# Attention with decay and a cosine feed-forward on one core: the order of all operations taken from a written table, buffers given out in that order

## The chip, the core and the metric

The kernel runs on one core of a Trainium2 chip. A core has a matrix engine (TensorE, PE in the profile, with its weight loads as PEld), a vector engine (VectorE, DVE), a scalar engine (ScalarE, ACT), a general engine (GpSimd, POOL) and a queue that starts transfers (SyncE, SP). Every engine runs its own list of instructions strictly in the order in which they were issued, and waits by semaphores for the others. The metric is the time of one execution on the device in microseconds, the median of several runs.

## What is computed

64 attentions (8 batches, 8 heads, 576 positions, 64 columns each) with a decay from a running sum of log f, a causal mask and a softmax; then a two-layer feed-forward over all 4608 tokens.

```python
scores = scale * np.matmul(q, k.transpose(0, 1, 3, 2))
cum = np.cumsum(np.log(np.clip(f, 0.0001, 1.0)), axis=-1)
scores = np.where(causal, -1000000000.0, scores + cum[..., :, None] - cum[..., None, :])
attn = np.exp(scores - scores.max(-1)); attn = attn / (attn.sum(-1) + 1e-09)
x = (attn @ v)                      # to 4608 x 512
h = x @ w_in                        # w_in 512 x 2048
out = (h * np.cos(h)) @ w_out       # w_out 2048 x 512
```

## The kernel before

**Stages.** Heads are taken two at a time: 32 pairs, four to a batch. A pair's scores come as row blocks of 128, in three groups of blocks, each in a bank of PSUM. For each block DVE adds the mask and takes the row's extreme (L826, L987), ACT takes the exponential and the row's sum (L836, L992), and ACT and DVE write the weights as a high and a low half-precision part (L1009, L1013). A transfer turns these parts over (L1018, the transposes pt<-PS), and PE multiplies them with the values: "PV", L1042, in two halves of 320 and 256 positions. The first four pairs (batch 0) go another way: scores in full f32 (L818), turned over by PE (L789), copied out of PSUM to `pt` (L777 on ACT, L778 on DVE, whichever the planner took), multiplied on PE (L863) and turned back (L888). Pairs 4 to 7 have f32 scores too (L973).

**Feed-forward.** A unit is half a batch (320 or 256 positions), 16 units in all. Its first product, gemm1 (L1072), makes four chunks `c` of four blocks of twelve matmuls each; ACT takes each block out of PSUM (L1078). Per chunk follow DVE L1087 and L1089, the sine on ACT (L1091), DVE L1093, the cast to the high part on ACT (L1100) and the low part g = h - high: L1101 on DVE, or L1102 on POOL. The second product, gemm2 (L1118), sums 48 matmuls for each of four blocks of the output; ACT scales it (L1124) and a transfer writes it.

**Weights.** Both weight matrices come in as 32 pieces of 512 KB, as 64-bit numbers. For each piece DVE puts an f32 together in three steps (L617, L621, L625), ACT takes the squares for a bound (L636), and once a group's scale is known ACT writes the high part (L646) and DVE the low part (L653; `on_pool`, L648, is the same on POOL, but `POOLW = ()` lets no matrix use it).

**What sets the order.** Nothing is issued as it is written. Each operation is an `Op` with an engine, a cost and the operations it depends on; 4219 of them. `Plan.forward` runs a planner with those costs and picks, on each engine, the ready operation with the smallest due time. It runs twice, then `shift` adds to each group's time a number of the table `SHIFT`, and it runs a last time; where an operation has an alternative engine (`alt`), the earlier runs choose. A ring of buffers (`Plan.ring`) hands out its tiles in the order in which the program text asks for them: a tile waits for all operations of the tile that had its place, and for the first operation of the tile asked for before it. In the first 200 us of the plan (`FILL`) the planner puts matmuls of constants into the gaps it sees on PE ("pads", L1186: `ones` and `mask`, 448 columns, result unused): 158 of them. Four numbers (`HOLDV`, `HOLDW`, `HOLDR`, `HOLDX`) hold some loads back in the plan.

Of the kernel before, what the change touches and what calls it, by code (L numbers as in the profile page):

```python
# [40 lines left out]
POOLW = ()  # L41
SLQ, SLW, SLG = 1.0, 50.0, 0.0
# [1 line left out]
HOLDV, HOLDW, HOLDR, HOLDX = 0.0, 0.0, 25.0, 25.
# [2 lines left out]
ROUNDS = 2
AHEAD = 15
# [1 line left out]
FILL, PAD = 200, 448  # L50
SWITCH = 6.0
# [1165 lines left out]
```

## Time and profile before

| | |
|---|---|
| time, three runs | 1071.93 us median (1070.89 to 1072.18) |
| span of the profiled execution | 1071.4 us, which is 0.5 us under that median |
| PE, DVE, ACT, POOL busy | 98%, 77%, 78%, 14% of the span |
| table loads on ACT (1283 ns each) | 93 |
| pads on PE (L1186) | 158, at 2.3 to 113.8 us, 34.5 us of busy time |
| first matmul of gemm1 (L1072) | starts at 114.29 us |

How to read it: a row of the windows view gives, for a stretch of the span, how long each engine was busy, the granted TensorE clock as a share of full speed, and the load on the transfer engines. A row of the timeline gives the start, the length and in square brackets the idle time before it, with what ended it. A row of the groups view gives, for one line of the kernel, the busy time of all its instructions (overlapping ones counted once) and the mean length of one.

### The profile page before, as it was taken

Reading aid. Unit: us, or ns where it says so; the run is one execution under the profiler, and the core shown is the slowest. Engines: PE = TensorE matmul, PEld = TensorE weight load, DVE = VectorE, ACT = ScalarE, POOL = GpSimd, SP = SyncE. Lnnn points to the kernel's source line nnn. Section 1 sums busy time; section 2 is a strip of 40 time slices with the busy share of each in tenths; the row PEclk is TensorE's granted clock in tenths of the full one; section 3 lists DMA queues with packets and bytes.
Section 4 is the critical chain, followed back from the end, with each engine's and each line's share of the span. In section 5 each row is a group of like instructions: output and inputs, shape, how many; then the busy total and the mean of one; then the engine's idle time right before and its main releaser. Section 6 shows DMA issues by size and latency. Waiting matters only on the chain. (4 is left out here: it accounts for less than half of the span.)

```text
span 1071.4 us, 23498 instructions
## 1 busy us (share of the span) xinstructions
PE 1050.1 (98%) x8975; PEld 841.6 (79%) x8975; DVE 819.7 (77%) x1801; ACT 832.2 (78%) x1739; POOL 155.3 (14%) x271
## 2 busy tenths in 40 slices
...
GB/s 267 309 284 109 99 135 102 126 162 158 180 152 147 139 142 167 149 101 159 182 154 144 127 148 167 169 129 130 178 144 144 134 142 75 85 59 21 7 20 20
DMA packets 256280, 146.37 MB, mean 137 GB/s; under 512 B 223337, under 2 KB 231529, under 8 KB 256169
## 3 DMA queue, kind: packets, MB, share of 16 engines
...
## 5 line engine op out<-in xcount | busy, mean ns | idle before, releaser
L1118 PE MATMUL hp<-g,W2s 128*128 128x256 f16 (+1 forms) x3072 | 390.9, 287 | 0.6 <-DVE W2s L653 0.4
L1072 PE MATMUL hp<-xh,W1s 128*128 128x256 f16 (+1 forms) x2048 | 380.4, 286 | 1.1 <-ACT h L1078 1.1
L1118 PEld LDWEIGHTS <-W2s 128*128 128x128 f16 x3072 | 297.9, 98 | 78.0 <-issue 0.8
L1072 PEld LDWEIGHTS <-W1s 128*128 128x128 f16 x3072 | 295.9, 98 | 78.6 <-issue 1.7
L1072 PE MATMUL hp<-xl,W1s 128*128 128x256 f16 (+1 forms) x1024 | 292.6, 286 | 0.0
L1013 DVE SCALAR_TENSOR_TENSOR PS<-pa,ri,PS 128x576 f16<-128x576 f32 (+2 forms) x280 | 140.7, 544 | 32.1 <-ACT PS L1009 31.3
L992 ACT ACTIVATE pa<-pa,nb 128x576 f32<-128x576 f32 (+2 forms) x280 | 141.1, 506 | 19.8 <-DVE nb L987 18.6
L987 DVE CUSTOM_DVE_ANT_0 pa<-pa,mask 128x576 f32<-128x576 f32 (+2 forms) x280 | 131.5, 513 | 31.8 <-PE pa L976 26.1
L1009 ACT ACTIVATE PS<-pa,ri 128x576 f16<-128x576 f32 (+2 forms) x280 | 134.1, 545 | 15.0 <-DMA pt<-PS 9.7
L1078 ACT ACTIVATE h<-hp 128x320 f32<-128x320 f32 (+1 forms) x256 | 101.3, 416 | 36.6 <-PE hp L1072 36.0
L1093 DVE TENSOR_TENSOR h<-h,r 128x1280 f32<-128x1280 f32 (+1 forms) x64 | 89.1, 1392 | 41.4 <-ACT r L1091 41.2
L997 POOL TENSOR_SCALAR ri<-L 128x1 f32<-128x1 f32 (+1 forms) x168 | 46.8, 279 | 410.4 <-ACT pa L992 404.9
L921 POOL TENSOR_TENSOR QK<-stage,QK 64x576 fp32r<-64x576 f32 x46 | 77.3, 1680 | 170.5 <-issue 116.4
L1091 ACT ACTIVATE r<-r,halfpi,m_inv 128x1280 f32<-128x1280 f32 (+1 forms) x64 | 86.2, 1347 | 18.8 <-DVE r L1089 18.3
L1101 DVE TENSOR_TENSOR g<-h,g 128x1280 f16<-128x1280 f32 (+1 forms) x62 | 84.2, 1358 | 14.1 <-ACT g L1100 13.7
L1087 DVE TENSOR_SCALAR r<-h,m_a 128x1280 int32<-128x1280 f32 (+1 forms) x64 | 56.8, 888 | 49.3 <-ACT h L1078 48.3
L1089 DVE SCALAR_TENSOR_TENSOR r<-r,m_b,h 128x1280 f32<-128x1280 int32 (+1 forms) x64 | 91.3, 1426 | 0.7
L975 PE MATMUL pa<-QK 128*128 128x288 f32 (+4 forms) x288 | 90.3, 330 | 1.5 <-DVE PS L1013 1.5
L1100 ACT CAST g<-h 128x1280 f16<-128x1280 f32 (+1 forms) x64 | 74.2, 1159 | 15.1 <-DVE h L1093 14.9
L1124 ACT ACTIVATE ot<-hp,m_o 128x320 f32<-128x320 f32 (+1 forms) x64 | 32.3, 504 | 65.9 <-PE hp L1118 50.4
L1042 PEld LDWEIGHTS <-vv 128*64 128x64 f16 x1512 | 69.4, 111 | 16.9 <-issue 14.2
L1042 PE MATMUL pa<-pt,vv 128*64 128x256 f16 (+2 forms) x1512 | 78.8, 256 | 3.7 <-DMA pt<-PS 3.4
...
## 6 DMA issues: line engine op xcount, KB each, us to landing
...
```

The lines of the kernel that those rows point to most:

```text
L975: T.matmul(c, hi[:, 0, isl], hi[:, 1, d], start=True, stop=False)
L987: op("DVE", c_dve(w) + 0.008, lambda view=view, ib=ib, o=o, w=w, mk=mk, c=c: V.tensor_tensor_reduce(out=view(ib, o, w), in0=view(ib, o, w) ...
L992: op("ACT", c_act(w, True, 2), lambda view=view, ib=ib, o=o, w=w, c=c: A.activation(view(ib, o, w), view(ib, o, w), AF.Exp, bias=nb.get()[ ...
L1009: op("ACT", c_act(w, True, 1), lambda view=view, ib=ib, o=o, w=w, c=c, out_=out_: A.activation(out_(0), view(ib, o, w), AF.Copy, scale=ri. ...
L1013: op("DVE", c_dve(w) + 0.06, lambda view=view, ib=ib, o=o, w=w, c=c, out_=out_: V.scalar_tensor_tensor(out_(1), view(ib, o, w), ri.get()[: ...
L1042: T.matmul(d, vv.get()[:, jb, hd, kv], m, start=first and x == 0, stop=last and x == 2)
L1072: T.matmul(hp.get()[:, 0:w_], WS_[1][:, at(1, 4 * c + cb), w, fs], x.get(), start=(n == 0), stop=(n == 11))
L1078: op("ACT", c_act(w_, True), lambda hp=hp, k=k: A.activation(h.get()[:, k, 0:w_], hp.get()[:, 0:w_], AF.Copy, scale=float(2.0 ** -24)), re ...
L1089: op("DVE", c_dve(N) + 0.045, lambda: V.scalar_tensor_tensor(fl(r), fl(r).bitcast(I32), b1.get()[:, c:c + 1], fl(h), op0=ALU.mult, op1=ALU ...
L1091: op("ACT", c_act(N, aps=2), lambda: A.activation(fl(r), fl(r), AF.Sin, scale=inv.get()[:, c:c + 1], bias=halfpi), reads=[inv], writes=[r] ...
L1093: op("DVE", c_dve(N), lambda: V.tensor_tensor(fl(h), fl(h), fl(r), op=ALU.mult), reads=[r], writes=hk, prio=pr)
L1118: T.matmul(po.get()[:, 0:w_], WS_[2][:, at(2, 4 * c + k), w, msl], gh.get()[:, i, k, 0:w_], start=(n == 0), stop=(n == 47))
```

## The change

`SHIFT`, `rank`, `backward`, `forward`, `shift`, the model of the clock and the latencies are gone. A table `ORDER` of 4219 words takes their place: each word is the number of an operation; an `a` behind it takes the alternative engine; `+8` puts eight pads ahead of it. `order` walks it. A ring's tile is now given out when its first operation is reached in the table, so the order within a ring can differ from the order of the text. The holds are no longer read. PV may now have pads (`fill`), and `POOLW = (1, 2)` lets the low parts of both weight matrices run on POOL where the table says so.

```diff
-POOLW = ()
-SLQ, SLW, SLG = 1.0, 50.0, 0.0
+POOLW = (1, 2)
-HOLDV, HOLDW, HOLDR, HOLDX = 0.0, 0.0, 25.0, 25.
+HOLDV, HOLDW, HOLDR, HOLDX = 0.0, 0.0, 0.0, 0.0
-SHIFT = {
-    0: 2.6, 1: 50.9, 2: -45.6, 6: -4.6, 8: 39.7, 9: -8.9, 11: 124.1, 12: 13.5, 14: -37.1, 24: 47.5, 25: 4.9, 26: 33.8, 27: 46.2,
...
+ORDER = """
+3 201 0 4 6 421 30 55 127 95 16 176 22 202 203 7 204 8 422 423 205 424 9 425 65 17 56 196 211 10 57 11 58 12 23 18 177 59 13 178 128 66 20
+179 1 67 180 292 197 307 68 31 19 198 69 199 200 21 32 75 24 25 96 26 293 97 27 294 5 28 60 129 295 308 90 296 2 309 181 45+8 310 186 213
...
     def ring(self, name, make):
-        old = self.rings.setdefault(name, [])
-        b = Buf(make)
-        if len(old) >= BUFS[name]:
-            b.wait = old[len(old) - BUFS[name]]
-        b.prev, b.name = old[-1] if old else None, name
-        old.append(b)
-        return b
+        return Buf(make, name=name)
...
     def order(self):
-        self.rank()
...
-        self.shift()
-        return self.forward(0.0)[0]
...
+        done, rings, out = set(), {}, []
+        for word in ORDER.split():
+            k, _, pads = word.partition("+")
+            o = self.ops[int(k.rstrip("a"))]
+            assert o.deps <= done and o.id not in done, word
+            for r in o.tiles:
+                used = rings.setdefault(r.name, [])
+                if r not in used:
+                    assert len(used) < BUFS[r.name] or not used[-BUFS[r.name]].left, word
+                    used.append(r)
+                r.left -= 1
+            done.add(o.id)
+            out.append((int(pads or 0), o.fill, o.alt[2] if "a" in k else o.fn))
+        assert len(out) == len(self.ops)
+        return out
...
             op("PE", sum(3 * c_mm((i1 - i0) * (P - c0)) for _, _, i0, i1, c0 in jobs) + 0.3, mm, reads=[*(T2, T3)[half], *vp_], writes=[pv],
-               prio=pr + 0.6)
+               prio=pr + 0.6, fill=lambda pv=pv: pv.get()[:, 0:PAD])
...
     with tc.manual_schedule():
-        for o in seq:
-            for _ in range(o.pads):
-                T.matmul(o.fill(), ones, mask[:, 0:PAD], start=True, stop=True)
-            o.fn()
+        for pads, fill, fn in seq:
+            for _ in range(pads):
+                T.matmul(fill(), ones, mask[:, 0:PAD], start=True, stop=True)
+            fn()
```

No matmul of the computation is added or removed. What changes in the counts: pads 158 to 27 (91 ahead of the first scores become 8); table loads on ACT 93 to 75; the 15 copies out of PSUM that DVE did (L778) all go to ACT (L777); the low parts of g on POOL 2 to 30; four of the 16 low parts of w_in go to POOL (two instructions each); of the two subtractions that prepare the scores of later pairs, POOL does 28 in place of 59 (L921, L922), DVE the rest. Three places show it.

VectorE, in the scores of the first pairs (L826 is the mask and row extreme, two rows for one; `pa` a bank of scores, `hp` a bank with blocks turned over, `pt` where they are copied to). Before:

```order
L826 ISA pa_369,nb<-pa_369,mask 128x448
L826 ISA nb 128x1
L778 COPY pt_391<-hp 128x384
L826 ISA pa_369,nb<-pa_369,mask 128x64
L826 ISA nb 128x1
L778 COPY pt_391<-hp 128x384
```

Now the copies stand on ScalarE (line 611 of the changed kernel is L777 of the profile before, 670 is L836, 470 is L636), between the exponentials of the same pairs:

```order
L470 ACTIVATE g,am_107<-W2s 128x512
L611 COPY pt_302<-hp 128x512 x2
L670 ACTIVATE PS_84,L<-pa_274,nb 128x576
L470 ACTIVATE h,ma<-W1s 128x512
L611 COPY pt_325<-hp 128x384
L670 ACTIVATE PS_85,L<-pa_264,nb 128x320
```

The DVE list has no such copy any more; between two softmax steps of these pairs stand weight pieces alone.

TensorE, at the first PV of batch 1, the fifth PV in the list (its first row is the 64x64 one). Before, 288 matmuls of gemm1 and 108 of gemm2 stand ahead of it:

```order
L1118 LDWEIGHTS W2s
L1118 MATMUL hp<-g,W2s 128x320
L1042 LDWEIGHTS vv
L1042 MATMUL pa_2263<-pt_2128,vv 64x64
L1042 LDWEIGHTS vv
L1042 MATMUL pa_2263<-pt_2226,vv 64x64
```

Now (952 is L1118, 807 is L973, 876 is L1042) 384 of gemm1 and 156 of gemm2 stand ahead of it, and one more group of scores between:

```order
L952 LDWEIGHTS W2s
L952 MATMUL hp<-g,W2s 128x320
L807 MATMUL pa_2402<-stage 128x320
L807 MATMUL pa_2402<-stage 128x192
L876 LDWEIGHTS vv
L876 MATMUL pa_2408<-pt_2154,vv 64x64
```

So this PV moved back by 144 matmuls of the two products.

GpSimd, behind its start (L592 is L758, clearing; 484 and 485 are the two steps of a low part of w_in, L650 and L651 before; 831 is L997, the softmax's small scale; 936 is L1102, a low part of g). Before, up to 204 us this list held constants, clearing and L997 alone. Now:

```order
L484 TENSOR_TENSOR W1s<-W1s,s_100 128x512
L485 TENSOR_TENSOR W1s<-W1s 128x512
L592 MEMSET stage 68x64 x2
L831 TENSOR_SCALAR ri<-L 128x1
L831 TENSOR_SCALAR ri<-L 128x2 x2
L831 TENSOR_SCALAR ri<-L 128x1
L936 TENSOR_TENSOR g<-h,g 128x1280
```

These are the last of four pairs of 484 and 485 and the first low part of g; all four pairs stand ahead of it.

More of the change, by code (lines that the diff above doesn't have):

```diff
@@ L40 @@
 CH = {1: 1, 2: 2}
[L41 to L42 removed]
+POOLW = (1, 2)
 LEAD = 2.5
[L44 removed]
+HOLDV, HOLDW, HOLDR, HOLDX = 0.0, 0.0, 0.0, 0.0
 NHP = 3
 N32, NQ = 4, 8
[L47 to L48 removed]
 EARLY = 2
[L50 to L51 removed]
+PAD = 448
 TWO_PI = 2.0 * np.pi
@@ new lines @@
+2211 2189 2193 2208 2506 2197 2190 2200 2206 2201 2209 2191 2212 2202 2730 2207 2519 2203 2932 2213 2536 2550 2214 2562 2520 2537 2204 2521
+2215 2205a 2733 2563 2538 2216 2433 2566 2773 2551 2771 2933 2570 2552 2567 2772 2539 2774a 2553 2767 2434 2217 2572 2571 2554 2775 2555
+2580 2218 2810 2734 2573 2853 2581 2435 2177 2735 2540 2556 2219 2523 2736 2582 2557 2768 2524 2568 2558 2564 2541 2737 2769 2542 2559 2543
+2583 2569 2544 3153 3072 2545 2574 2546 2604 2584 2547 2575 2549 2608 2605 2560 2576 2548 2740 2752 2741 2586 2561 2753 2742 2754 2609 2577
@@ L183, with __init__ @@
+4110 4137 4111 4129 4112 4113a 4130 4131 4138 4132 4139 4140 4169 4153 4170 4133 4134 4167 4154 4171 4168 4187 4172 4185 4188 4181 4186 4159
+4182 4183 4160 4157 4184 4189 4141 4190 4158 4191 4142 4192 4143 4193 4175 4176 4144 4194a 4177 4147 4145 4178 4146 4148 4161 4149 4162 4150
+4163 4195 4164 4151 4152 4165 4207 4179 4166 4201 4180a 4208 4196 4197 4202 4203 4204 4198 4205 4206 4209 4210 4199 4200 4213 4214 4211 4215
+4212 4216 4217 4218
+"""
 class Buf:
-    def __init__(self, make=None, parent=None):
-        self.make, self.parent, self.t = make, parent, None
-        self.last, self.readers, self.parts = None, [], {}
-        self.ops, self.wait, self.prev, self.closed, self.name = [], [], None, False, None
+    def __init__(self, make=None, parent=None, name=None):
+        self.make, self.parent, self.name, self.t = make, parent, name, None
+        self.last, self.readers, self.parts, self.left = None, [], {}, 0
@@ L207 @@
 class Op:
-    __slots__ = ("eng", "cost", "size", "table", "fn", "prio", "deps", "succ", "n", "ready", "id", "t", "alt", "due", "port", "first", "moving", "bank", "fill", "end", "pads", "hold")
-LAT = {("ACT", "ACT"): 0.034, ("ACT", "DVE"): 0.131, ("ACT", "PE"): 0.17, ("ACT", "POOL"): 0.18, ("ACT", "SP"): 0.13,
-       ("DVE", "ACT"): 0.13, ("DVE", "DVE"): 0.134, ("DVE", "PE"): 0.155, ("DVE", "POOL"): 0.155, ("DVE", "SP"): 0.12,
-       ("PE", "PE"): 0.0, ("PE", "ACT"): 0.197, ("PE", "DVE"): 0.197, ("PE", "SP"): 0.19, ("PE", "POOL"): 0.2,
-       ("POOL", "ACT"): 0.085, ("POOL", "DVE"): 0.05, ("POOL", "PE"): 0.1, ("POOL", "SP"): 0.1, ("POOL", "POOL"): 0.05}
@@ L215 @@
-SHARED = {"DVE": "POOL", "POOL": "DVE"}
-DMQ, DMC = int(1.35 * 360e3), int(0.5 * 360e3)
-PADG, PADE, PE0 = 0.3, 0.0, 2.5
-VACT = 2
-T_DGE, T_DMA0, T_DMA1, DMA_BW, T_TABLE = 0.5, 0.65, 0.9, 360e3, 1.28
-class Clock:
-    W, HIGH, LOW, SLOW = 3.413, 0.49, 0.36, 2.0
-    def __init__(self):
-        self.k, self.busy, self.warm = 0, 0.0, False
-    def close(self):
-        u = self.busy / self.W
-        self.warm = u > self.HIGH or (self.warm and u > self.LOW)
-        self.k, self.busy = self.k + 1, 0.0
-    def run(self, t, cost, share=1.0):
-        while t >= (self.k + 1) * self.W:
-            self.close()
-        while True:
-            f = 1.0 if self.warm else self.SLOW
-            room = (self.k + 1) * self.W - t
-            if cost * f < room:
-                self.busy += cost * share
-                return t + cost * f
-            self.busy += room / f * share
-            t, cost = t + room, cost - room / f
-            self.close()
-    def pad(self, a, b):
-        n = 0.0
-        while a < b:
-            while a >= (self.k + 1) * self.W:
-                self.close()
-            e = min(b, (self.k + 1) * self.W)
-            self.busy += (e - a) * (0.9 if self.warm else 0.5)
-            n += (e - a) / ((1.0 if self.warm else 2.0) * (PAD / 2400 + 0.003))
-            a = e
-        return int(n)
@@ L261 @@
+    __slots__ = ("eng", "cost", "size", "table", "fn", "prio", "deps", "tiles", "id", "alt", "port", "moving", "fill", "hold")
+DMQ, DMC, DMA_BW = int(1.35 * 360e3), int(0.5 * 360e3), 360e3
+T_DGE = 0.5
+VACT = 2
 class Plan:
     def __init__(self):
-        self.ops, self.rings, self.first = [], {}, 0.0
+        self.ops = []
     def ring(self, name, make):
-        old = self.rings.setdefault(name, [])
-        b = Buf(make)
-        if len(old) >= BUFS[name]:
-            b.wait = old[len(old) - BUFS[name]]
@@ L278, in op @@
         o.eng, o.cost, o.size, o.table, o.fn, o.prio, o.alt, o.id = eng, cost, size, table, fn, prio, alt, len(self.ops)
-        o.port, o.first, o.moving, o.fill, o.pads, o.hold = port, self.first, moving, fill, 0, hold
-        o.bank = []
-        deps = {}
-        for b in reads:
+        o.port, o.moving, o.fill, o.hold = port, moving, fill, hold
+        deps = set()
+        for b in (*reads, *writes):
             if b.last is not None:
-                deps[b.last.id] = b.last
+                deps.add(b.last.id)
         for b in writes:
-            if b.last is not None:
-                deps[b.last.id] = b.last
-            for r in b.readers:
-                deps[r.id] = r
-        for b in (*reads, *writes):
-            r = b.root()
-            assert not r.closed, r.name
-            if r.wait:
-                r.wait.closed = True
-                for w in r.wait.ops:
-                    deps[w.id] = w
-                o.bank += r.wait.ops
-            if r.prev is not None and r.prev.ops:
-                deps[r.prev.ops[0].id] = r.prev.ops[0]
-            r.ops.append(o)
+            deps.update(r.id for r in b.readers)
         for b in reads:
@@ L304, in op @@
             b.last, b.readers = o, []
-        deps.pop(o.id, None)
-        o.deps, o.succ, o.n, o.ready = list(deps.values()), [], len(deps), 0.0
-        for d in o.deps:
-            d.succ.append(o)
+        o.deps = deps - {o.id}
+        o.tiles = list({id(r): r for r in (b.root() for b in (*reads, *writes)) if r.name}.values())
+        for r in o.tiles:
+            r.left += 1
         self.ops.append(o)
         return o
-    def rank(self):
-        t = 0.0
-        for o in self.ops:
-            o.due = 1e9
-        for o in sorted((o for o in self.ops if o.eng == "PE"), key=lambda o: (o.prio, o.id)):
-            o.due = t
-            t += o.cost
-        for o in reversed(self.ops):
-            c = T_DMA0 + o.size / DMA_BW + T_DMA1 if o.eng == "SP" else o.cost + 0.15
-            for x in o.succ:
-                o.due = min(o.due, x.due - c)
@@ L325, in backward @@
-    def backward(self, end):
-        free, avail, future, n = {}, {}, [], {}
-        late = {}
-        for o in self.ops:
-            free.setdefault(o.eng, 0.0)
-            avail.setdefault(o.eng, [])
-            n[o.id], late[o.id] = len(o.succ), 0.0
-            if not o.succ:
-                heapq.heappush(future, (0.0, o.id, o))
-        t, left = 0.0, len(self.ops)
-        while left:
-            while future and future[0][0] <= t + 1e-9:
-                o = heapq.heappop(future)[2]
-                heapq.heappush(avail[o.eng], (-end[o.id], o.id, o))
-            nxt = []
-            for e, q in avail.items():
-                if q and free[e] <= t + 1e-9:
-                    o = heapq.heappop(q)[2]
-                    left -= 1
-                    free[e] = t + o.cost
-                    stop = t + (T_DMA0 + o.cost + o.size / DMA_BW if e == "SP" else o.cost)
-                    o.due = -stop
-                    for d in o.deps:
-                        late[d.id] = max(late[d.id], stop + (T_DMA1 if d.eng == "SP" else LAT[d.eng, e]))
-                        n[d.id] -= 1
-                        if not n[d.id]:
-                            heapq.heappush(future, (late[d.id], d.id, d))
-                if q:
-                    nxt.append(free[e])
-            if future:
-                nxt.append(future[0][0])
-            t = max(t, min(nxt, default=t))
@@ L359, in order @@
-    def order(self):
-        self.rank()
-        base = [(o.eng, o.cost, o.fn) for o in self.ops]
-        for k in range(ROUNDS):
-            if k:
-                self.backward(end)
-            for o, x in zip(self.ops, base):
-                o.eng, o.cost, o.fn = x
-            out, end = self.forward()
-        self.shift()
-        return self.forward(0.0)[0]
-    def shift(self):
-        group = {}
-        for o in self.ops:
-            k = group.setdefault((o.fn.__code__.co_firstlineno, o.prio), o.id)
-            o.due, o.alt = o.t + o.first + SHIFT.get(k, 0.0), None
@@ new lines, in order @@
+    def order(self):
+        done, rings, out = set(), {}, []
[3 more added lines that the diff above has]
+            assert o.deps <= done and o.id not in done, word
+            for r in o.tiles:
+                used = rings.setdefault(r.name, [])
[7 more added lines that the diff above has]
+        return out
@@ L653, in split @@
         op("DVE", c_dve(512) + 0.056, lambda: V.scalar_tensor_tensor(lo, wide_of(w, k), s, hi, op0=ALU.mult, op1=ALU.subtract),
-           reads=[sb, *hb], writes=[lb, *wb], prio=pr, alt=("POOL", 2 * c_pool(512), on_pool, SLW) if w in POOLW else None)
+           reads=[sb, *hb], writes=[lb, *wb], prio=pr, alt=("POOL", 2 * c_pool(512), on_pool) if w in POOLW else None)
     ma = const.tile([P, NF], F32, name="ma")
@@ L924, in sub @@
         def sub(f, reads, writes):
-            op("DVE", c_dve(S), lambda: f(V), reads=reads, writes=writes, prio=pr, alt=("POOL", c_pool(S) + 0.03, lambda: f(G), SLQ))
+            op("DVE", c_dve(S), lambda: f(V), reads=reads, writes=writes, prio=pr, alt=("POOL", c_pool(S) + 0.03, lambda: f(G)))
         vv = ring("vv", [P, 5, 2, 2, D], F16)
```

161 lines of the change are left out of this document (89 added, 72 removed), and 167 rows, old and new, of tables (ORDER, SHIFT).

## The prediction

> **What bounds the kernel now.** First the page, for the shares:
>
> ```profile
> PE 1050.1 (98%) x8975; PEld 841.6 (79%) x8975; DVE 819.7 (77%) x1801; ACT 832.2 (78%) x1739; POOL 155.3 (14%) x271
> ```
>
> PE is the bound on average, but part of its busy time is no work: the 158 pads, and matmuls at half clock. So I cut the span into stages with the windows view (busy time of each engine, granted clock, transfer load):
>
> ```profile
> 0.00:21.00 21.00, 18.71 (x91) 9.40 (x92) 12.45 (x23) 7.37 (x17) 4.87 (x24) 1.00 0.81 264
> 21.00:57.00 36.00, 32.28 (x199) 23.73 (x199) 33.14 (x99) 27.96 (x81) 0.85 (x6) 0.99 0.94 296
> 57.00:114.30 57.30, 55.33 (x378) 46.00 (x377) 55.06 (x172) 41.81 (x124) 2.46 (x13) 0.97 0.60 175
> 114.30:150.00 35.70, 35.70 (x281) 25.94 (x280) 35.10 (x91) 31.54 (x70) 1.88 (x7) 1.00 0.58 125
> 150.00:187.40 37.40, 34.32 (x277) 25.44 (x276) 36.51 (x83) 36.87 (x75) 3.05 (x8) 1.00 0.47 114
> 187.40:206.00 18.60, 15.31 (x74) 9.98 (x74) 12.61 (x26) 10.77 (x21) 1.56 (x6) 0.63 0.53 126
> 206.00:1068.00 862.00, 858.30 (x7685) 701.12 (x7683) 634.83 (x1314) 675.40 (x1355) 140.60 (x208) 1.00 0.58 126
> 1068.00:1071.40 3.40, 0.13 (x2) 0.00 (x0) 0.00 (x0) 0.47 (x1) 0.00 (x0) 0.84 0.11 39
> ```
>
> Read the third column as PE, the fifth as DVE. From 206 us on PE lacks 3.7 us of 862, while DVE and ACT have over 180 us to spare: that stage is PE's and no order shortens it by more than 3.7. The tail of 3.3 us is the last transfer. Everything else is ahead of 206 us, and there **DVE** is the full engine: 33.14 of 36.00, 55.06 of 57.30, 35.10 of 35.70, 36.51 of 37.40. The same view for the pads alone (line L1186):
>
> ```profile
> 0.00:21.00 21.00, 18.71 (x91) 9.23 (x91) 1.00 0.81 264
> 21.00:57.00 36.00, 8.57 (x41) 3.81 (x40) 0.99 0.94 296
> 57.00:114.30 57.30, 7.18 (x27) 2.88 (x27) 0.97 0.60 175
> ```
>
> Up to 114.3 us, where gemm1 starts, PE was busy 18.71 + 32.28 + 55.33 = 106.3 us, of which 34.5 were pads: 71.9 us of work, so 42.4 us of the ramp are lost. The pads cost nothing themselves; they lie in gaps that DVE leaves. Behind that, the timeline of PE and the clock in steps of its 3.4 us grid:
>
> ```profile
> 189.66 1.92 PE L1042 MATMUL pa<-pt,vv 128*64 128x64 f16 x23 [2.30 <-DMA pt<-PS]
> 192.62 5.88 PE L973 MATMUL pa<-stage 68*128 68x448 f32 x12 [1.03 <-DMA stage<-in_dram]
> ...
> 53.20:56.60 3.40, 2.33 (x10) 1.62 (x10) 2.34 (x6) 1.80 (x6) 0.15 (x1) 1.00 1.04 220
> ...
> 186.30:189.70 3.40, 1.10 (x11) 0.57 (x11) 3.40 (x5) 2.85 (x4) 0.30 (x2) 1.00 0.62 120
> 189.70:193.10 3.40, 2.37 (x24) 1.92 (x24) 3.40 (x6) 1.79 (x3) 0.00 (x0) 0.50 0.79 184
> 193.10:196.50 3.40, 3.40 (x9) 2.20 (x8) 1.69 (x3) 0.94 (x1) 0.00 (x0) 0.50 0.92 175
> ...
> 199.90:203.30 3.40, 3.40 (x14) 1.96 (x13) 2.62 (x5) 1.56 (x7) 0.15 (x1) 0.50 0.44 172
> ```
>
> PE waits at the fifth PV, the clock falls, and it stays at half for four steps, 189.7 to 203.3. Lost there: idle 37.40 - 34.32 = 3.1 up to 187.4, 18.60 - 15.31 = 3.3 behind, and half of the 12.6 us busy at half clock, 6.3. Sum **12.7 us**. So 1071.4 is about 1009.3 us of work at full clock + 42.4 + 12.7 + 3.7 + 3.3.
>
> **The change part by part.** The prices of DVE's instructions, from the groups view:
>
> ```profile
> L778 DVE COPY pt<-hp 128x512 f32<-128x512 f32 (+2 forms) x15 | 7.9, 536 | 1.1 <-ACT pt L777 0.8 <-PE hp L789 0.3
> L653 DVE SCALAR_TENSOR_TENSOR W1s<-W1s,s 128x512 f16<-128x512 f32 x16 | 11.9, 744 | 0.0
> L621 DVE SCALAR_TENSOR_TENSOR W2s<-g,W2s 128x512 int32<-128x512 int32 x16 | 10.9, 684 | 0.1
> L714 DVE TENSOR_REDUCE vmx<-stage 128x1 f32<-128x640 f32 x24 | 19.3, 813 | 1.8 <-DMA stage<-in_dram 1.7
> L1089 DVE SCALAR_TENSOR_TENSOR r<-r,m_b,h 128x1280 f32<-128x1280 int32 x32 | 49.4, 1542 | 0.3
> L1013 DVE SCALAR_TENSOR_TENSOR PS<-pa,ri,PS 128x576 f16<-128x576 f32 (+2 forms) x280 | 140.7, 544 | 32.1 <-ACT PS L1009 31.3
> ```
>
> *The first gemm1.* Ahead of it on PE stands the same work as before. On DVE, of what it needs, 15 copies are gone (-7.9) and 5 low parts of weights are later or on POOL (-3.7); 7 more steps of L621 and L625 (7 x 0.68 = 4.8), 2 short L617 (about 0.8), 2 reductions L714 (1.6) and some small scale work (about 1.5) have come ahead. Net -2.9 us. The copies go to ACT, +7.4 there; ACT was busy 77.1 of these 114.3 us, so the cover stands, and if it were gone the price is those 7.4 us.
>
> *POOL beside DVE.* Up to 204 us POOL had no tensor work. Now four low parts of w_in (two instructions each) run in the ramp, and three or four low parts of g follow before the fifth PV. What DVE pays is seen in two pairs of the timeline:
>
> ```profile
> 473.64 1.92 POOL L922 TENSOR_TENSOR QC<-stage,QK 64x576 fp32r<-64x576 f32 x1
> 474.33 2.31 DVE L1089 SCALAR_TENSOR_TENSOR r<-r,m_b,h 128x1024 f32<-128x1024 int32 x1
> ...
> 471.55 2.13 POOL L1102 TENSOR_TENSOR g<-h,g 128x1024 f16<-128x1024 f32 x1 [13.18 <-ACT g L1100]
> 472.42 0.80 DVE L987 CUSTOM_DVE_ANT_0 pa<-pa,mask 128x576 f32<-128x576 f32 x1
> ```
>
> An L1089 over 1024 columns, at 4/5 of the 1542 ns above or some 1.23 us, took 2.31 beside POOL: +1.1 for 1.2 us together. An L987, which reads PSUM, took 0.80 us there, and its mean is
>
> ```profile
> L987 DVE CUSTOM_DVE_ANT_0 pa<-pa,mask 128x576 f32<-128x576 f32 x56 | 42.9, 765 | 12.5 <-PE pa L976 11.1 <-PE pa L973 1.2
> ```
>
> so almost nothing. The price is between 0 and 0.9 us for each us of POOL. A low part of w_in on POOL has no row; bounded by the L1102 above (1024 columns, 2.13 us) for each of its instructions, and by half of that, it takes 2.1 to 4.3 us; I take 2.6. Four make 10.4 us. About half of DVE's work in the ramp is of the kind that is slowed, so I take 0.4: **+4 us** (0 to +9). First gemm1: 114.3 - 2.9 + 4 = about 115.4, within 111 to 121.
>
> Behind each low part on POOL's list stands the softmax's small scale L997, for which DVE's reciprocal and ACT's L1009 wait: up to 2.6 us later for a pair, covered by the gemm blocks that PE has ahead of that pair's PV (next paragraph).
>
> *The fifth PV.* It moved back by 144 matmuls, priced by the chain's last pieces:
>
> ```profile
> 1005.37 26.08 PE hp L1118 x192
> ```
>
> 26.08/192 = 0.136 us each at 320 columns: 19.6 us more work on PE ahead of the wait, and with the scores between about 21. DVE must do more ahead of it too: 7 steps of the mask with their readings (4.3), 5 of L1013 (2.5), two steps of L1087 and L1089 (4.6), 3 reductions (2.4), scales (2.5), less the copies (7.9) and 3 low parts (2.2): +6, and another 4 us of contention with the low parts of g (0 to 9). The wait was 2.3 us; 21 - 10 leaves 11 us of cover against the 6.4 us of idle time in this stretch. With no idle step the clock does not fall. So all 12.7 go in the likeliest case; at the upper bounds of the contention (9 + 9) the cover is about 2 and half of the 12.7 stays.
>
> *What costs nothing.* 28 low parts of g and 18 fewer table loads (18 x 1.28 = 23 us of ACT) lie mostly behind 206 us, where DVE is busy 634.83 and ACT 675.40 of 862: PE covers them. The rings given out in the order of issue add no work. The pads save nothing: DVE's work, not PE's, ends the ramp.
>
> *The start of the queue SP.* The load of f was issued second, and now stands behind a write that needs POOL's clearing of `pt`:
>
> ```profile
> 1.55 0.58 SPq L586 DMA_DIRECT2D vv<-in_dram  x1
> ...
> 3.27 2.05 POOL L580 MEMSET pt<- 64x1152 f32 x2
> ```
>
> The first of the two clearings ends at about 4.3 us, so f is issued some 3 us later. Scores and softmax of the first pairs start later by up to that, while weight pieces that came first feed DVE: 0 to 3 us, I take 0.8.
>
> **Sum.** 1071.4 - 2.9 + 4 + 0.8 - 12.7 = 1060.6 us of span, and the runs' median was 0.5 above the span: **1061 us**, 1.0% less.
>
> **The rivals.**
> *The clock in the ramp* (slower). The ramp's scores are f32 matmuls on 68 rows. In the rows above, 193.1 to 196.5 is full of them (3.40 busy), and the clock did not come back in the two steps behind; one step with 2.33 us busy at 53.2 was enough to lose it. With 19 pads in place of 67 behind the first scores, PE stands idle there more and may run at half clock. PE has 71.9 us of work between 21 and about 115 us, so 22 us of room; each us at half clock takes half a us: up to 44 us at half clock it is hidden, at 44 + 2 x 10.4 = 65 us the gain is eaten, and with the whole ramp at half clock gemm1 starts at 21 + 144 = 165 and the kernel takes about 1110. Against it: the row 57.00 to 114.30 held its clock at 0.97 in the mean with 7.18 us of pads and 2.0 us idle, work of the same kind. Chance 0.15.
> The Trainium skill, "TensorE: Matmul & The Clock Gate", Part 1, says that the clock halves after at least one idle window of about 3.4 us and returns after one busy window. By that rule neither gap here (2.30 and 1.03 us) halves it and fewer pads cost one start-up window, so this rival would fall away. The trace goes against it on both sides: 1.10 and 2.33 us busy of 3.40 were lost, and 3.40 of 3.40 did not bring it back.
> *Nothing moves* (the table does not do what it should). If PE finds at each place of the new order another wait of the same size, or contention takes its upper bound, 1061 + 10 = 1071, 1066 to 1074. Against it: the cover of 11 us at the one decisive wait. Chance 0.11.
> *More goes.* DVE's own idle time ahead of 114.3 us is 8.6 + 2.9 + 2.2 = 13.7; an order made operation by operation may close half of it (6.8), contention may be nil (4), late gaps may close (3 of 3.7): 1061 - 14 = 1047. Against it: the first 8.6 wait for the first loads. Chance 0.21.
>
> **How the numbers follow.** Forecast 1061 (1053 to 1066): 0.53; more goes (1043 to 1053): 0.21; nothing moves: 0.11, of which 0.07 lies within 0.2% (2.1 us, about what a measurement of this kernel can tell from no change) and 0.04 below; the clock: 0.15. Faster 0.53 + 0.21 + 0.04 = 0.78, same 0.07, slower 0.15. The range leaves out a few hundredths below 1045 and about a tenth above 1082, part of the clock's cases.
>
> **What would show it.** Right: gemm1 starts at 111 to 121 us, PE has no gap over 1 us between there and 206, and the clock is 1.00 throughout that stretch; DVE is busy over 90% from 21 us to there; from 206 us on PE is as full as before. Wrong: the clock at 0.50 for over 44 us ahead of gemm1; a first gemm1 ahead of 108 us (DVE's idle time closed); L617 to L625 and L653 over 20% longer than before (contention mis-sized); idle PE in the stage behind 206 us.

## The result, and the profile after

The changed kernel takes **1064.69 us** (median of four runs, 1063.21 to 1066.05); the kernel before took 1071.41 beside it. The ratio is 0.9937, with a 95% interval of 0.9922 to 0.9951: 0.6% less. The forecast was 1061, 1.0% less. Runs that were slow as a whole are left out of all ratios and ranges here (one of e1, below, took 1773 us).

A run's time lies 1.7 us above its own span: the profiled execution of the changed kernel, 1064.1 us of span, took 1065.79. So the 1071.4 us of span before belong to a time of about 1073.1, above the four timed runs. The profiled spans differ by 7.3 us, the medians by 6.7; the accounts below are of the profiled executions.

The shares of the page of the changed kernel, and its windows view, cut as before; columns are stretch, length, busy time of PE, PEld, DVE, ACT and POOL, granted clock, transfer load, GB/s:

```profile
PE 1025.7 (96%) x8844; PEld 834.7 (78%) x8844; DVE 811.1 (76%) x1785; ACT 816.3 (77%) x1736; POOL 197.8 (19%) x276
```

```profile
0.00:21.00 21.00, 0.00 (x0) 0.10 (x1) 14.05 (x23) 8.76 (x21) 4.98 (x25) 1.00 0.77 257
21.00:57.00 36.00, 32.28 (x147) 23.44 (x146) 27.74 (x84) 22.28 (x71) 0.59 (x4) 0.81 0.88 272
57.00:114.30 57.30, 54.72 (x369) 46.26 (x369) 54.18 (x176) 50.05 (x149) 8.47 (x17) 0.94 0.67 194
114.30:150.00 35.70, 35.70 (x286) 26.94 (x286) 35.08 (x85) 32.90 (x64) 7.61 (x9) 1.00 0.56 127
150.00:187.40 37.40, 37.40 (x309) 28.98 (x308) 35.18 (x80) 34.02 (x73) 10.31 (x13) 1.00 0.45 98
187.40:206.00 18.60, 17.84 (x136) 14.13 (x135) 13.83 (x41) 14.35 (x37) 3.19 (x7) 1.00 0.85 192
206.00:1060.50 854.50, 847.40 (x7607) 694.85 (x7606) 631.08 (x1302) 653.44 (x1327) 162.68 (x201) 1.00 0.56 127
1060.50:1064.10 3.60, 0.33 (x3) 0.04 (x1) 0.00 (x0) 0.48 (x1) 0.00 (x0) 0.90 0.11 36
```

Three things are to be seen. From 114.3 to 206 us PE lacks 0.76 us where it lacked 6.4, and the clock is 1.00: the stretch of the fifth PV is repaired. Ahead of it the clock is at 0.81 and 0.94 where it was 0.99 and 0.97, and DVE is busy 27.74 of 36 us where it was 33.14. And from 206 us on PE lacks 7.1 us of 854.5 where it lacked 3.7. The first gemm1 (L906 is L1072 of the profile before) stands in the view of that line; its fourth figure is the first start:

```profile
L906 PE MATMUL hp<-xh,W1s x2048: 269/292/314, 117.4 to 1026.4; 128*128 128x256 f16 x95, 128*128 128x320 f16 x92
```

So the profiled span, 1064.1, comes about as 1071.4 + 3.2 (gemm1 at 117.4 in place of 114.3) - 5.6 (idle time between there and 206) - 6.3 (half clock there) + 3.4 (idle time behind 206) - 2.0 (rest). Of that rest 1.8 is the first matmul of each later score pair: 288 of them took 90.3 us at 330 ns before, 88.5 at 323 now.

```profile
L975 PE MATMUL pa<-QK 128*128 128x288 f32 (+4 forms) x288 | 90.3, 330 | 1.5 <-DVE PS L1013 1.5
```

```profile
L809 PE MATMUL pa<-QK 128*128 128x288 f32 (+4 forms) x288 | 88.5, 323 | 1.7 <-DVE PS L847 1.4 <-DVE xl L884 0.2
```

(The first row is of the kernel before, the second of the changed one, both from 206 us on.)

### The profile page after: what moved, and what is told of

Its sections match the earlier page's. It is cut to its first block, busy times and chain, and to the rows that moved or that the text cites. A ratio compares the mean times of both kernels' runs of the same rounds, so it can differ in the third digit from the quotient of the medians.

```text
span 1064.1 us, 23115 instructions
## 1 busy us (share of the span) xinstructions
PE 1025.7 (96%) x8844; PEld 834.7 (78%) x8844; DVE 811.1 (76%) x1785; ACT 816.3 (77%) x1736; POOL 197.8 (19%) x276
## 5 line engine op out<-in xcount | busy, mean ns | idle before, releaser
L952 PE MATMUL hp<-g,W2s 128*128 128x320 f16 (+1 forms) x3072 | 387.6, 286 | 0.3 <-ACT h L912 0.3
L906 PE MATMUL hp<-xh,W1s 128*128 128x256 f16 (+1 forms) x2048 | 380.0, 286 | 1.9 <-ACT ot L958 1.0
L906 PEld LDWEIGHTS <-W1s 128*128 128x128 f16 x3072 | 298.0, 98 | 78.2 <-issue 2.6
L906 PE MATMUL hp<-xl,W1s 128*128 128x256 f16 (+1 forms) x1024 | 292.6, 286 | 0.0
L847 DVE SCALAR_TENSOR_TENSOR PS<-pa,ri,PS 128x576 f16<-128x576 f32 (+3 forms) x280 | 142.9, 543 | 40.1 <-ACT PS L843 39.5
L826 ACT ACTIVATE pa<-pa,nb 128x576 f32<-128x576 f32 (+4 forms) x280 | 141.8, 508 | 37.0 <-DVE nb L821 34.9
L821 DVE CUSTOM_DVE_ANT_0 pa<-pa,mask 128x576 f32<-128x576 f32 (+4 forms) x280 | 132.9, 506 | 23.2 <-PE pa L810 21.6
L843 ACT ACTIVATE PS<-pa,ri 128x576 f16<-128x576 f32 (+3 forms) x280 | 136.4, 537 | 16.8 <-DMA pt<-PS 11.4
L912 ACT ACTIVATE h<-hp 128x256 f32<-128x256 f32 (+1 forms) x256 | 102.8, 416 | 48.7 <-PE hp L906 42.6
L831 POOL TENSOR_SCALAR ri<-L 128x1 f32<-128x1 f32 (+1 forms) x168 | 55.2, 329 | 386.4 <-ACT pa L826 378.4
L936 POOL TENSOR_TENSOR g<-h,g 128x1280 f16<-128x1280 f32 (+1 forms) x30 | 80.8, 2693 | 248.5 <-ACT g L934 248.5
L925 ACT ACTIVATE r<-r,halfpi,m_inv 128x1280 f32<-128x1280 f32 (+1 forms) x64 | 86.3, 1348 | 26.1 <-DVE r L923 25.3
L809 PE MATMUL pa<-QK 128*128 128x288 f32 (+4 forms) x288 | 88.5, 323 | 1.7 <-DVE PS L847 1.4
L921 DVE TENSOR_SCALAR r<-h,m_a 128x1280 int32<-128x1280 f32 (+1 forms) x64 | 54.2, 847 | 47.1 <-ACT h L912 45.9
L810 PE MATMUL pa<-QC 68*128 68x288 f32 (+4 forms) x288 | 76.5, 304 | 0.0
L750 ACT CAST QK<-stage 128x1152 fp32r<-128x1152 f32 x48 | 55.2, 1151 | 16.1 <-PE pa L809 8.5
```

Source lines behind the costliest of these rows:

```text
L809: T.matmul(c, hi[:, 0, isl], hi[:, 1, d], start=True, stop=False)
L810: T.matmul(c, co[0:68, 0, isl], co[0:68, 1, d], start=False, stop=True)
L821: op("DVE", c_dve(w) + 0.008, lambda view=view, ib=ib, o=o, w=w, mk=mk, c=c: V.tensor_tensor_reduce(out=view(ib, o, w), in0=view(ib, o, w) ...
L826: op("ACT", c_act(w, True, 2), lambda view=view, ib=ib, o=o, w=w, c=c: A.activation(view(ib, o, w), view(ib, o, w), AF.Exp, bias=nb.get()[ ...
L843: op("ACT", c_act(w, True, 1), lambda view=view, ib=ib, o=o, w=w, c=c, out_=out_: A.activation(out_(0), view(ib, o, w), AF.Copy, scale=ri. ...
L847: op("DVE", c_dve(w) + 0.06, lambda view=view, ib=ib, o=o, w=w, c=c, out_=out_: V.scalar_tensor_tensor(out_(1), view(ib, o, w), ri.get()[: ...
```

## The experiments

Twelve kernels, on three chips, each beside the kernel before on the same chip. Runs of one kernel lay 4 to 15 us apart there, the kernel before included (most between 1070 and 1079), so the ratios carry intervals of 0.2 to 0.4% each way, and I read the mechanism from one profiled execution of each. Nine are edits of the changed kernel, b1 to b3 of the kernel before. All are edits of the table, in which the order of the kernel before can be written too, word for word. The table is wrapped wider in them, so their lines stand 10 (b1 to b3: 9) lower than in the changed kernel: L642 there is L652. "DVE" is its busy and idle time ahead of the first gemm1, "half" the time ahead of it in which PE's work ran at half clock (by the record, and by the length of matmuls where there is none), "late" PE's idle time from 206 us to 3.5 us before the end.

| kernel | first gemm1 | half | DVE busy, idle | late | span | ratio to before (95%) |
|---|---|---|---|---|---|---|
| before | 114.3 | 3.4 | 100.6, 13.6 | 3.7 | 1071.4 | 1 |
| changed | 117.4 | 20.5 | 99.0, 18.4 | 7.1 | 1064.1 | 0.9937 (0.9922 to 0.9951) |
| e1 early start | 116.5 | 25.0 | 98.0, 18.5 | 7.5 | 1062.7 | 0.9941 (0.9919 to 0.9964) |
| e2 91 pads first | 120.6 | 30.7 | 99.3, 21.3 | 4.6 | 1064.9 | 0.9927 (0.9899 to 0.9954) |
| e3 both, 75 pads | 118.8 | 30.7 | 97.6, 21.1 | 5.4 | 1061.9 | 0.9891 (0.9859 to 0.9923) |
| f1 both, 97 pads | 117.4 | 20.5 | 98.0, 19.4 | 6.4 | 1064.3 | 0.9953 (0.9924 to 0.9981) |
| f2 and in the ramp | 116.8 | 13.7 | 98.1, 18.6 | 9.6 | 1067.3 | 0.9914 (0.9883 to 0.9945) |
| e4 no pads | 145.6 | 89 | 100.5, 45.1 | 9.3 | 1095.2 | 1.0100 (1.0061 to 1.0140) |
| e5 copies on DVE | 131.3 | 45 | 106.0, 25.3 | 10.1 | 1081.0 | 1.0046 (1.0017 to 1.0075) |
| e6 low parts on DVE | 118.8 | 22 | 100.5, 18.3 | 6.8 | 1065.5 | 0.9931 (0.9911 to 0.9950) |
| l1 late waits | 115.6 | 15 | 98.8, 16.8 | 10.3 | 1067.9 | 0.9984 (0.9957 to 1.0011) |
| b1 before, 16 pads | 113.7 | 0 | 100.5, 13.3 | 3.4 | 1065.5 | 0.9953 (0.9933 to 0.9973) |
| b2 before, copies on ACT | 114.6 | 0 | 95.1, 19.5 | 4.8 | 1072.5 | 1.0037 (1.0008 to 1.0067) |
| b3 both of these | 115.0 | 0 | 95.0, 20.0 | 2.4 | 1066.3 | 0.9986 (0.9958 to 1.0014) |

One row bounds what a start of gemm1 can tell: l1 has the ramp of the changed kernel unaltered, and yet gemm1 at 115.6 and 15 us at half clock in place of 117.4 and 20.5. Two executions of one ramp can lie some 2 us apart. The column "late" scatters more: the changed kernel and its eight edits other than l1 have one order from 206 us on, and lie between 4.6 and 10.1. The four executions with the order of the kernel before lie between 2.4 and 4.8.

### Half clock at the fifth PV: b1

```diff
-... 921 638 663 922 937 949 601 930 ...
+... 921+11 638 663 922 937+5 949 601 930 ...
```

> The kernel before, its order written as a table word for word, with 11 pads ahead of the fifth PV and 5 ahead of the scores behind it. Of the 12.7 us that the prediction lets go there, 6.3 are half clock and 6.4 idle time. Pads can save the first part and not the second. If the size of 6.3 is right: 1065 to 1067 where the kernel before takes 1071.4, the clock 1.00 from 187 to 206. If the half clock cost nothing (DVE was behind anyway, and a slower PE only waits less): 1071 +- 1.

Timeline of PE in b1 (L867 is L1042, L798 is L973, L1009 the pads):

```profile
186.50 2.24 PE L1009 MATMUL pa<-mask,ones 128*128 128x448 bf16 x11
188.67 0.22 PE L867 MATMUL pa<-pt,vv 128*64 128x64 f16 x1
189.51 1.08 PE L867 MATMUL pa<-pt,vv 128*64 128x64 f16 x23 [0.62 <-DMA pt<-PS]
190.52 1.12 PE L1009 MATMUL pa<-mask,ones 128*128 128x448 bf16 x5
191.95 3.05 PE L798 MATMUL pa<-stage 68*128 68x448 f32 x12 [0.31 <-DMA stage<-in_dram]
194.83 6.68 PE L943 MATMUL hp<-g,W2s 128*128 128x320 f16 x48
```

The PV's 23 matmuls take 1.08 us where they took 1.92, the twelve score matmuls 3.05 for 5.88, the 48 behind them 6.68 for 9.17: the clock held, though PE comes to the data no earlier. The span is 1065.5, 5.9 less, against a term of 6.3; 0.6 of the 5.9 was there already at gemm1. By the ratio it is 5.0 us (2.9 to 7.2). Sixteen instructions that compute nothing bring nearly as much as the whole new order.

### The ramp: e1, e2, e3, f1, f2

The start of the table in e1, which also brings the loads of q (128, 31, 96) ahead of weight pieces and the running sum (9 to 11) ahead on DVE:

```diff
-3 201 0 4 6 421 30 55 ... 202 203 7 204 8 422 423 205 424 9 425 65 17 56 196 211 10 57 11 58 12 ...
+6 3 201 0 4 1 421 30 55 ... 202 203 7 8 204 9 10 11 422 423 205 424 425 12 13 128 31 96 65 ...
```

> Edit: in the new table the load of f is issued first, the four writes of the running sum and the first loads of q come ahead of later weight pieces, DVE does the running sum as soon as its data is there, and PE does the first reduction of batch 0's value scale (one matmul) behind the first three score groups in place of ahead of them. Nothing else. Theory 1 (the ramp is longer than forecast because its scores start late): the first scores start at about 20 us in place of 27.67, DVE's idle time up to the first gemm1 falls from 18.4 by 3 to 5 us, gemm1 starts at 113 to 115 in place of 117.5 and the kernel takes 1060 to 1062. Theory 2 (the clock at half in the ramp is what costs): the scores start early but still cold, gemm1 moves by under 1 us, 1064 +- 1. Theory 3 (DVE has the weights to do meanwhile and loses nothing): no change, 1064 +- 1, with DVE's idle time moved, not gone.

> Edit: 91 pads ahead of the first score group (in place of 8), as before the change, and the one matmul of batch 0's value scale behind the first three score groups; all else as in the new table. Theory 1 (late scores): the data for the first scores is there at 27.6 us as before, so no more than 1 us is gained by the clock, 1063 to 1065. Theory 2 (cold clock): the clock is at 1.00 from 27 us on, the 13.65 us at half clock between 29 and 43 us go, gemm1 starts some 3 us earlier (114 to 115), 1060 to 1062. Theory 3 (DVE full anyway): 1064 +- 1.

> Edit: the early start and 75 pads ahead of the first score group together. If late scores and cold clock both cost, the two gains add: gemm1 at 110 to 113, 1057 to 1060. If only one of them costs, the time is that of the one run alone, within 1 us. If DVE is full anyway, 1064 +- 1.

Timelines of PE, first of e1, then of the kernel with 97 pads (f1):

```profile
22.86 5.81 PE L642 MATMUL pa<-g 68*128 68x320 f32 x12 [17.38 <-DMA g<-cum_d]
...
33.13 5.91 PE L642 MATMUL pa<-g 68*128 68x288 f32 x12 [2.28 <-ACT PS L660]
```

```profile
22.86 3.02 PE L642 MATMUL pa<-g 68*128 68x320 f32 x12 [0.43 <-DMA g<-cum_d]
...
33.83 5.91 PE L642 MATMUL pa<-g 68*128 68x288 f32 x12 [6.64 <-ACT PS L660]
```

In the kernel before, the first scores started at 21.02, at full clock:

```profile
21.02 2.97 PE L818 MATMUL pa<-g 68*128 68x288 f32 x12
```

The change had put them at 27.67, 6.65 us later. In e1 they start 4.8 us earlier again, at 22.86, but gemm1 moves by 0.9 us only, within the 2 us above, and DVE's idle time not at all. In f1 they also run at full clock (3.02 us for 5.81); then PE waits 6.64 us for ACT, the clock falls, and gemm1 stands where it stood.

> Edit: the early start with 97 pads ahead of the first score group in place of 75, so that the last pad ends when the data of the first scores lands (22.8 us; with 75 there were 4.4 us of waiting between, and 12 score matmuls then took 5.67 us where they took 2.97 before the change). Theory 2 (half clock in the ramp costs): the 12 take about 3.0 us, the half clock that lasted to 46 us goes, PE gains some 10 us of work by 46 us, gemm1 starts at 112 to 115 in place of 118.6, 1056 to 1059 where the version with 75 took 1061.6. Theory 3 (DVE's list sets the ramp): gemm1 at 117 to 119, 1061 to 1062.

> Edit: as the run with 97 pads, and 9 and 7 more pads ahead of two score groups in the ramp (they fill waits for ACT's exponential, 2.3 us at about 31 and 1.4 at about 69 us). Theory 2 (half clock costs, also the 6.8 us of it at 70 to 77): another 1 to 3 us, gemm1 at 110 to 113, 1054 to 1057. Theory 3: as the run with 97 pads, or 1 to 2 us longer, since the pads delay two groups of scores.

What DVE waits for up to 117 us, in f1 (L441 are the first steps of a weight piece):

```profile
DVE W1s L441 <- DMA h<-in_dram: 4.9, 2, 4.4
DVE W2s L441 <- DMA g<-in_dram: 4.3, 1, 4.3
```

The waits for weight pieces grew to 9.2 us. In the changed kernel they are 6.4 in the same view:

```profile
DVE pa L660 <- PE pa L652: 3.7, 7, 1.0
DVE W2s L451 <- DMA g<-in_dram: 3.6, 2, 3.1
DVE W1s L451 <- DMA h<-in_dram: 2.8, 2, 1.8
```

In e1 they are 8.4. So the late scores (theory 1) alone do not set gemm1: what comes earlier on the queue makes the weights later, and what DVE no longer waits for PE (5.8 us in the changed kernel, 3.6 in e1) it waits for those. Nor does full clock for the first scores (theory 2) bring gemm1 forward; but in f1 the clock falls in the wait behind them, and the ramp has as much half clock as without the edit (20.5 us). e2 missed its aim: its pads ended at 22.5 us, the scores' data came at 27.3, and in that wait of 4.83 us the clock fell for 23.9 us in place of 13.7. f2 has the least half clock of the five (13.7) and gains 0.6 us at gemm1. e3 has the lowest ratio of all kernels, but not by an earlier gemm1 (118.8); its interval meets that of the changed kernel, so I do not call it faster than that.

### No pads: e4

> Edit: the 27 pads of the new table are left out, all else the same. The prediction's own claim (pads save nothing, DVE ends the ramp): 1064 +- 1, with more half clock in the ramp but gemm1 at 117 to 118. Theory 2 (cold clock costs): up to 30 us more at half clock ahead of gemm1, gemm1 2 to 6 us later, 1066 to 1070.

PE's timeline in e4 and its gemm1:

```profile
28.26 13.17 PE L642 MATMUL pa<-g 68*128 68x320 f32 x28 [3.28 <-DMA g<-in_dram]
41.22 3.41 PE L613 MATMUL hp<-eyef,PS 128*128 128x128 f32 x15
...
47.02 1.12 PE L613 MATMUL hp<-eyef,PS 128*128 128x128 f32 x4
```

```profile
L896 PE MATMUL hp<-xh,W1s x2048: 270/292/472, 145.6 to 1057.6; 128*128 128x256 f16 x95, 128*128 128x320 f16 x92
```

A score matmul takes 13.17/28 = 0.47 us, where 2.97/12 = 0.25 is full clock. It stays at half to 83.6 us, where the first record of a full clock stands, and is at half again from 87.0 to 121.1: 55 + 34 = 89 us. gemm1 starts 28 us later, and the ratio is 1.0100 against 0.9937, some 17 us. This profiled execution is one of the two longest (1097 us; the other four runs, from which the ratio comes, took 1080 to 1088), so the 17 is the price, and the 28 and 89 us are this execution's. Both expectations were too low. Which of the 27 pads do it was not tested by itself; e3, where the clock was at half up to six pads at 44.7 us, points at these (timeline of PE):

```profile
42.62 2.29 PE L642 MATMUL pa<-g 68*128 68x288 f32 x4 [0.28 <-ACT PS L660]
44.70 2.39 PE L1008 MATMUL hp<-mask,ones 128*128 128x448 bf16 x6
46.93 0.60 PE L613 MATMUL hp<-eyef,PS 128*128 128x128 f32 x4
```

Four transposes take 0.60 us behind these pads; in e4, at the same place without them, 1.12, and the clock is back 37 us later. In the changed kernel's own profiled execution, however, the clock was back before these six, at 42.8 us. The prediction's sentence that the pads save nothing falls: going from 158 to 27 cost little, but those 27 hold off some 17 us.

### The copies: e5 and b2, b3

e5 puts an "a" behind the words of the 15 copies (51 to 51a, and so on), b2 takes it off in the order of the kernel before; b3 is b2 with the pads of b1.

> Edit: the 15 copies out of PSUM go back to VectorE (the same 15 as before the change), at their places in the new table; all else as in the new table. The prediction's term: VectorE has 7.9 us more ahead of the first gemm1, which starts up to 7.9 us later than 117.5, and the time is up to 8 us longer (1069 to 1073), since VectorE was over 90 % busy. The rival: VectorE has 18.4 us idle ahead of gemm1 in the new kernel, the copies fall into waits, gemm1 at 117 to 120 and 1064 to 1067.

> The kernel before, its order word for word, with the 15 copies out of PSUM on ScalarE in place of VectorE and nothing else. The prediction's term: VectorE has 7.9 us less ahead of the first gemm1; it starts at 106 to 109 in place of 114.3, and since the fifth PV waits for VectorE's list too, its wait goes in part: 1060 to 1066. The rival (PE's chain of score groups, or ScalarE with 7.4 us more, sets the ramp): gemm1 at 112 to 116 and 1069 to 1073.

> The kernel before with both: the 15 copies on ScalarE, and 16 pads at the fifth PV and the scores behind it (which alone took the profiled span from 1071.4 to 1065.5). If the two are separate prices they add: 1054 to 1061. If the copies' gain is the same time as the pads' (the wait at the fifth PV is gone either way): the better of the two alone, within 1 us.

Windows up to gemm1, first b2, then e5:

```profile
21.00:57.00 36.00, 33.56 (x203) 23.85 (x202) 30.70 (x92) 29.39 (x86) 1.00 (x6) 1.00 0.93 295
57.00:114.30 57.30, 54.47 (x377) 45.28 (x376) 51.88 (x163) 45.19 (x134) 2.36 (x13) 1.00 0.59 176
```

```profile
21.00:57.00 36.00, 32.76 (x124) 22.58 (x124) 26.26 (x77) 18.82 (x57) 0.66 (x4) 1.00 0.83 259
57.00:131.20 74.20, 69.14 (x410) 58.20 (x409) 65.64 (x208) 51.66 (x149) 10.60 (x19) 0.84 0.57 162
```

One edit, two answers, neither of them the 7.9. In the old order DVE is freed of 5.5 us and idles 5.9 longer: gemm1 at 114.6, nothing gained (by the ratio something lost), and b3's span is about that of b1 (1066.3 and 1065.5). In the new order, giving them back costs 13.9 us at gemm1: 7.0 more of DVE's work and 6.9 more idle time, with 45 us at half clock in place of 20.5. By the ratios (1.0046 and 0.9937) that is some 12 us of time. A full DVE was no bound that a copy less would lift; but b2 gives the copies to ACT (busy 81.7 us up to 114.3, 77.1 before), so it does not tell a chain through PE from one through ACT. In the new order, where PE has only 27 pads, a copy more on DVE makes PE wait (2.5 us for the copied blocks); that the clock does the rest is read from the clock column, not tested.

### GpSimd beside VectorE: e6

> Edit: the four low parts of w_in that the new table gives to GpSimd go to VectorE (one instruction of 0.74 us each) at their places; all else as in the new table. The prediction's price for GpSimd beside VectorE in the ramp was +4 us (0 to 9): if it holds, gemm1 starts 1 us earlier than 117.4 (4 less, 3.0 more), 1063 to 1064. If there is next to no contention there (the rows of the changed kernel show VectorE's weight steps at 683 ns, as before): gemm1 1 to 5 us later, 1065 to 1069.

DVE does 1.5 us more ahead of gemm1 and gemm1 starts 1.4 us later. That is no sign of contention that came off, but within the 2 us of scatter it would not settle the matter. The changed kernel's rows do. Timeline, POOL's low part of w_in (L484, L485) and what DVE did meanwhile:

```profile
110.30 1.04 POOL L484 TENSOR_TENSOR W1s<-W1s,s 128x512 f32<-128x512 f32 x1 [1.23 <-ACT W1s L480]
111.42 1.16 POOL L485 TENSOR_TENSOR W1s<-W1s 128x512 f16<-128x512 f32 x1
```

```profile
110.52 0.34 DVE L821 CUSTOM_DVE_ANT_0 pa<-pa,mask 128x192 f32<-128x192 f32 x1
...
110.89 0.82 DVE L847 SCALAR_TENSOR_TENSOR PS<-pa,ri,PS 128x576 f16<-128x576 f32 x1
111.63 0.55 DVE L715 TENSOR_TENSOR xs<-hp,ri 128x384 f32<-128x384 f32 x1
```

DVE worked on PSUM (`pa`, `hp`), at its usual lengths, and so it is at nearly all of the 18.8 us that POOL spends on two-operand instructions up to 206 us; only two of DVE's were slowed by them, 0.9 us in all, both behind 180 us. The weight steps, of a kind with two operands in SBUF, lie elsewhere and keep their length (DVE's groups up to 117.5 us; 687 before):

```profile
L455 DVE SCALAR_TENSOR_TENSOR W1s<-h,W1s 128x512 int32<-128x512 int32 x16 | 10.9, 683 | 0.1
```

One step of a weight piece did meet POOL, and not where the prediction looked: at the start, beside the clearing of `pt` (timelines of DVE and POOL).

```profile
4.07 1.82 DVE L451 TENSOR_SCALAR W2s<-g 128x512 int32<-128x512 int32 x1 [3.13 <-DMA g<-in_dram]
```

```profile
3.20 2.06 POOL L414 MEMSET pt<- 64x1152 f32 x2
```

The other L451 take 0.42 us, this one 1.82: 1.4 us more. In e1 this step starts at 5.04 us, near the end of the clearing, and takes 0.84. In the kernel before, DVE waited for its first load while POOL cleared.

### The late waits: l1

PE's list at one of the seven places (3314 a PV that waited 1.1 us, 3117 and 3115 blocks of gemm1):

```diff
-3342 3314 3117 3115 3131
+3342 3117 3115 3314 3131
```

> Edit of the new table on PE alone: at seven places behind 190 us where PE waited 0.5 to 1.2 us (6.6 us in all), the operation that waited goes behind one to three operations that were ready. Theory (the waits are local, each operation merely stands too early on PE's list): PE's idle time from 206 us on falls from 7.1 to 2 or 3, the time is 4 to 5 us under that of the changed kernel. Rival (PE has caught up with VectorE's and ScalarE's lists there, and the waits come back at the next place): idle time 5 to 8, time as the changed kernel's, ratio 0.992 to 0.995.

The theory fails, and the waits come back, as the rival has it; the time is worse than the rival's numbers, too. Waits of PE from 186 us on in l1:

```profile
PE hp L896 <- ACT h L902: 2.7, 4, 0.9
PE pa L866 <- DMA pt<-PS: 1.4, 2, 1.2
PE hp L942 <- DVE g L925: 1.3, 1, 1.3
PE pa L797 <- DVE PS L837: 1.3, 1, 1.3
PE hp L942 <- ACT g L924: 1.2, 1, 1.2
```

Five of the seven waits went. At 222 us the block of gemm2 that I put ahead waited itself, 1.2 and 1.3 us for g (L924, L925); at 518 the PV waits 1.2 us three us later; and gemm1's readout (L902) is waited for 3.3 us in all, 0.7 before. Behind the two waits at 222 us the clock is at 0.50 for 3.4 us (223.5 to 226.9). Together 10.3 us in place of 7.1, which the scatter of "late" alone could give; but the ratio, 0.9984, is clear of the changed kernel's, and of 0.9931 for e6 on the same chip.

## Why the prediction was right, and where it was not

**The fifth PV** (-12.7): right in mechanism and nearly in size, -11.9. Its transposes, before and now (view of the line; first and last start):

```profile
L1018 SPq DMA_TRANSPOSE pt<-PS x3: 1430/1771/2702, 174.1 to 185.9; - x3
```

```profile
L852 SPq DMA_TRANSPOSE pt<-PS x4: 1437/2720/3576, 184.7 to 198.3; - x4
```

The last one is issued 12.4 us later (DVE's and ACT's work ahead; I had taken 10), and PE comes to the PV at 208.2 in place of 187.1, 21.1 us later (I had taken 21). At 3.7 us from issue to data, as before (185.9 to 189.66), 6 us of cover are left. b1 shows the half-clock part alone, 5.9 for 6.3 by the spans, 5.0 by the ratio. The idle part, 5.6 of 6.4, I read from the traces only; that PV can't be moved on PE alone, since the three open sums of gemm2 ahead of it wait for a g that DVE has not made yet.

**DVE's work ahead of gemm1** (-2.9) and **contention** (+4, 0 to 9): the first was right, the second mis-sized and put in the wrong place. Busy time fell by 1.6 in all. Without the 1.4 of the one step beside POOL's clearing, which the sum did not have, it would have fallen by 3.0. The low parts cost DVE nothing ahead of gemm1 and 0.9 us up to 206 us, not 8, because of where the table puts POOL's instructions; a mean share of slowed work (0.4) can't tell that. A low part on POOL took 1.04 + 1.16 = 2.2 us, in the bounds of 2.1 to 4.3, below the 2.6 taken. And "DVE is the full engine" was the step that failed in the ramp: b2 took 5.5 us off DVE and got nothing. 94.5% busy (88.20 of 93.30 us from 21 us on) is not a bound by itself; what bounds the ramp in its place stays open.

**The late start of f** (+0.8): mis-sized, and not what keeps gemm1 late. The first scores came 6.65 us later, not up to 3, and DVE's idle time ahead of gemm1 rose by 4.8, not 0.8; e1 and f1 took the late start away and it stayed. It is not the loads either: weight pieces are waited for 6.4 us against 2.7, but the first load 0.7 against 4.6, together 7.1 against 7.3. What rose are the waits for PE, 2.6 to 5.8, and for ACT, 1.4 to 3.4. Waits of DVE ahead of gemm1, before and now (three more rows of now stand in the section on the ramp):

```profile
DVE vv L587 <- DMA vv<-in_dram: 4.6, 1, 4.6
DVE pa L826 <- PE pa L818: 2.3, 3, 1.0
```

```profile
DVE xs L715 <- PE hp L697: 2.1, 1, 2.1
DVE pa L660 <- ACT pt L611: 1.6, 1, 1.6
```

L611 are the copies that now stand on ACT alone. How much of these waits is theirs, and how much PE's half clock, no run separates.

So the start of gemm1, 117.4 against 115.4, is in part luck: DVE's busy time came out 2.7 us under the sum, its idle time 4.0 above it.

**Pads and clock in the ramp.** The forecast that fewer pads cost little held (20.5 us at half clock, gemm1 within its 111 to 121; four runs with 94 to 132 pads have ratios of 0.9891 to 0.9953), though DVE was busy 88% from 21 us to 114, not the 90 that I had named. The sentence "the pads save nothing" did not. The rival's price was right in kind, its room too large: e4's 89 us at half clock and a start 28.2 us later give, at half a us for each, a room of 89 - 2 x 28.2 = about 33 us of half clock, not 44. With that e5 comes out as well: 45 - 33 = 12, half of it 6, and 7.0 of DVE's work, 13 us; measured 13.9. These are two executions, one of each, so the 33 is a rough estimate. The Trainium skill, "TensorE: Matmul & The Clock Gate", Part 1, lets the clock return after one busy window of about 3.4 us; in e4 it did not in 13.17 us without a gap.

**The stage behind 206 us** (0): +3.4, and I had named idle PE there as a sign of error. It cost most of the gap between 1061 and 1064.7; l1 shows that it is not a matter of single places. The 3.4 is one pair of executions; the ranges above, 2.4 to 4.8 and 4.6 to 10.1, show the same sign. What in the new order makes it stays open. That no order shortens this stage by more than its idle time did not hold either: the first matmuls of the score pairs took 1.8 us less.

Sum: gemm1 came 3.2 us later where the sum had 1.9 (1.3), 3.4 late, 0.8 of the stall left, 2.0 less in the rest (1.8 of it the cheaper scores): 3.5, and 1064.1 - 1060.6 is 3.5.
